# First query tiles of four batches ahead, then batch 0 by tiles of 128 queries, then twelve pairs: a sparse-attention and MLP kernel reordered

## The chip, the cores and the metric

The kernel runs on one core of a Trainium2 chip. Its time is the device time of one launch in microseconds (us): the median of three runs before the change is 282.17 us (280.68 to 282.51). A profile is one execution of the program; its span is counted from the first to the last instruction. TensorE is called PE here, VectorE DVE, ScalarE ACT and GpSimd POOL; SP is the queue that issues most DMAs. PE's weight loads have a row of their own, PEld, and run beside its matmuls.

## What is computed

Two parts follow each other: attention in which each query sees six chunks of 32 keys, and an MLP with a layer norm in front and a residual around it.

```python
# B, H, S, D = 4, 8, 768, 64; chunks of 32 keys, nc = 24
ub = sum(maximum(q * k_min, q * k_max), axis=-1)     # bound of each query against each chunk
ub = where(causal, ub, -1e9)
top_chunks = argsort(ub)[..., -6:]
scores = where(selected chunk and key <= query, q @ k.T / 8, -1e9)
x = softmax(scores) @ v                              # heads side by side: (4, 768, 512)
xn = (x - mean) / sqrt(var + 1e-6) * g_ln
out = x + maximum(xn @ w_ch1, 0) @ w_ch2             # 512 -> 2048 -> 512
```

A query in the first 128 positions has at most four chunks at or before it, so nothing is selected there: it sees all keys up to itself.

## The kernel before

**Tiling.** Queries and keys come in six tiles of 128 per batch. Heads are taken in pairs: 16 pairs, numbered 0 to 15, four to a batch, two heads of 64 channels side by side on 128 partitions. The queries of a batch form two halves of three tiles, r = 0 and r = 1. The MLP works on one half of one batch at a time: 384 rows.

**A pair's way.** q and k are turned so that channels lie on partitions. For batch 0 (pairs 0 to 3) PE does this with fp32 transposes against an identity (`turn`, line 236), half by half; for pairs 4 to 15 the load already brings 32x32 blocks and DVE turns them (line 229). `kbound` takes minimum and maximum of each chunk. `kdiag` puts them into a matrix with the two heads apart. `bounds` multiplies them with the queries on PE: for batch 0 in fp32 with the positive and negative parts of q (line 338), for the others with q split into two fp16 parts (line 325). `select` finds the seventh-largest bound of each row (DVE max instructions, line 356) and writes a 0/1 mask, `maskt` turns the mask on PE (line 366), and `mring` copies it under the queries: `QA`, `QB` hold q in 64 rows and the mask in the other 64, `KA`, `KB` hold k and constant rows of -61440 from `RT`, so that one matmul gives score and mask (`smm`, line 419). `sexp` is the exponential on ACT (line 427), `diag` cuts the diagonal blocks on POOL (line 434), `values` multiplies with v (line 450; v has a column of ones for the sum), `norm` divides on DVE (line 465).

**The MLP.** `pstat` and `centre` compute mean and variance and the centred fp16 rows on DVE (lines 480 to 492); `xt` turns them by a DMA transpose on SP's queue (line 509); `m1` is the first matmul, 16 groups of 128 hidden columns, two groups to a call (line 518); `relu` brings each to SBUF, nearly always on ACT (line 530); `m2` is the second, four calls of four matmuls to a tile of rows (line 543); `fin` scales, adds the residual and issues the store (line 552).

**Order.** The whole order is written out by hand in the string `ORDER`. Each engine and DMA queue takes its instructions in exactly that sequence; `a.b.c@n` calls function `a` with the numbers, and n picks an engine or a count. All PSUM tiles except those of `smm` and `m1` share four buffers (`ps_t`); `smm` and `m1` share two (`ps_m`).

**Fillers.** `busy` (line 117) issues matmuls whose result is overwritten by the next real one, in the calls of batch 0 and its MLP; `warm.11` (line 378) issues eleven such matmuls of 512 columns at the very start.

**Queues.** SP issues loads of q and k, stores, the DMA transposes of `xt` and the copies of `qring`. POOL issues the loads of v and of both weights (each weight in four parts, `w1` and `w2`). Before a weight load POOL writes one element of its target from `kc` (lines 172 and 176), so that the load follows that pair's `kbound`.

Of the kernel before, what the change touches and what calls it, by code (L numbers as in the profile page):

```python
# [10 lines left out]
ALU = mybir.AluOpType  # L11
# [8 lines left out]
def kernel(  # L20
# [19 lines left out]
    TR = NT // NR  # L40
# [19 lines left out]
    vap = ctx.enter_context(tc.tile_pool(name="vap", bufs=5))  # L60
# [3 lines left out]
    xp = ctx.enter_context(tc.tile_pool(name="xp", bufs=5))  # L64
    xcp = ctx.enter_context(tc.tile_pool(name="xcp", bufs=2))
    htp = ctx.enter_context(tc.tile_pool(name="htp", bufs=2))
# [8 lines left out]
    ident_b = const.tile([P, P], BF16, name="ident_b", tag="ident_b")  # L75
    causb = const.tile([P, NT - 1, 2, NCH], BF16, name="causb", tag="causb")
    causf = const.tile([P, NT - 1, 2, NCH], F32, name="causf", tag="causf")
    RT = const.tile([P, S], F16, name="RT", tag="RT")
    tiny = const.tile([1, 1], F32, name="tiny", tag="tiny")
    hsel = const.tile([P, 3, 2], F32, name="hsel", tag="hsel")  # L80
    mhalf = const.tile([P, TR], F32, name="mhalf", tag="mhalf")
    NK = 4
    QA = [ring.tile([P, S], F16, name=f"QA{i}", tag=f"QA{i}") for i in range(NK)]
    QB = [ring.tile([P, S], F16, name=f"QB{i}", tag=f"QB{i}") for i in range(NK)]
    KA = [ring.tile([P, S], F16, name=f"KA{i}", tag=f"KA{i}") for i in range(NK)]
    KB = [ring.tile([P, S], F16, name=f"KB{i}", tag=f"KB{i}") for i in range(NK)]
    NB = 3
    BD = [ring.tile([P, 2, 2, NCH], F32, name=f"BD{i}", tag=f"BD{i}") for i in range(NB)]
    BH = [ring.tile([P, 2, 2, 2, NCH], F16, name=f"BH{i}", tag=f"BH{i}") for i in range(NB)]
    NM = 3  # L90
    MN = [ring.tile([P, NT - 1, P], F16, name=f"MN{i}", tag=f"MN{i}") for i in range(NM)]
# [7 lines left out]
    st = [dict() for _ in range(NG)]  # L99
    hf = {}  # L100
    x_tiles = {}

    other = [0]
    fill = {P: (8, 16, 32), 240: (4, 8, 16), 122: (8, 16, 32)}
# [7 lines left out]
    def busy(o):  # L114
        w = o.shape[1]
        for _ in range((0, *fill[w])[other[0]]):
            nc.tensor.matmul(o, ident_b, causb.rearrange("p s h c -> p (s h c)")[:, 0:w], start=True, stop=True)  # L117

    def consts():
        make_identity(nc, ident_f)
# [10 lines left out]
        nc.gpsimd.memset(causb, 0.0)  # L133
        nc.gpsimd.affine_select(
            out=causb, in_=causb, compare_op=ALU.is_ge, fill=CAUSAL,
            base=P, pattern=[[P, NT - 1], [0, 2], [-CH, NCH]], channel_multiplier=1,
        )
        nc.vector.memset(hsel, 0.0)
        nc.scalar.activation(tiny, hsel[0:1, 0, 0:1], ACTF.Exp)
        nc.vector.memset(hsel[0:64, 0, 1:2], -KS)  # L140
        nc.vector.memset(hsel[64:P, 0, 0:1], -KS)
        nc.vector.memset(hsel[0:64, 1:3, 1:2], KS)
        nc.vector.memset(hsel[64:P, 1:3, 0:1], KS)
        for i in range(NM):
# [552 lines left out]
```

The softmax here doesn't subtract the row's maximum and nothing guards it: scores larger than these inputs give would overflow.

## Time and profile before

| what | value |
|---|---|
| median of three runs | 282.17 us |
| span of the profiled execution | 278.8 us |
| instructions | 6816 |
| HBM read, written | 27.53 MB, 6.29 MB |
| exponentials (line 427) | 96, 84.4 us busy on ACT |
| first MLP matmuls (line 518) | 512, 88.3 us busy on PE |
| second MLP matmuls (line 543) | 400, 93.0 us busy on PE |
| first and last start of line 518 | 45.9 us, 267.8 us |

Busy time is the time in which at least one instruction of a row was under way. Matmuls are pipelined: one of 384 columns shows 326 ns from start to end, but eight in a row take 1.30 us, so the pitch in the chain of waits is used for sums, not the mean duration of one. The median stands 3.4 us above the span.

### The profile page before, as it was taken

The numbers are of one execution on the slowest core, as the hardware profiler recorded it, in microseconds if no ns is written. First come the engines' busy times: TensorE is split into PE (matmuls) and PEld (weight loads), VectorE is DVE, ScalarE is ACT, GpSimd is POOL, SyncE is SP. The second block draws the span as 40 slices with busy tenths as digits, with TensorE's granted clock in tenths as the row PEclk, the third lists the DMA queues.
The fourth block names the chain that finished last, engine by engine and source line by source line (L and its number), as shares of the span: only waits on it lengthen the run. The fifth ranks groups of instructions, "written<-read, shape, count | busy, mean of one in ns | idle before, by whom it ended". The sixth has DMA issues, their size and how long they took to land.

```text
span 278.8 us, 6816 instructions
## 1 busy us (share of the span) xinstructions
PE 269.2 (97%) x2643; PEld 180.1 (65%) x2643; DVE 215.9 (77%) x632; ACT 177.9 (64%) x237; POOL 99.4 (36%) x170
## 2 busy tenths in 40 slices
PE   7989998999999999999999999999999999999994
PEld 3978986677556766666667766566666655555541
DVE  6888999899999989999999989898876665021212
ACT  3877997889947856758665787577777332413310
POOL 8615466847292034542262904220164000100100
PEclk9999999999999999999999999999999999999999
DMA  6989999989999995699614799455021012210202
GB/s 150 200 177 170 190 127 199 146 122 178 161 182 144 146 178 126 93 179 189 70 41 96 123 144 120 72 162 105 0 68 40 38 42 72 77 40 38 75 4 114
DMA packets 135745, 32.05 MB, mean 115 GB/s; under 512 B 127008, under 2 KB 132640, under 8 KB 135712
## 3 DMA queue, kind: packets, MB, share of 16 engines
q1 hardware_dynamic: 106320, 24.00, 44.3%
q0 software_dynamic: 29248, 7.34, 28.3%
q8 instruction: 21, 0.34, 0.5%
q10 hardware_dynamic: 144, 0.26, 0.3%
q14 instruction: 12, 0.10, 0.1%
HBM read 27.53 MB, written 6.29 MB: 121 GB/s over the span
## 4 chain that ended last, share of the span: by engine, by line
PE 87%; DVE 6%; DMA 3%; ACT 2%; issue 1%; SPq 1%; DVEq 0%; ACTq 0%
PE mm L518 30%; PE yp L543 30%; PE mm L419 11%; PE sm L450 6%; PE ub L325 3%; DMA xT<-xc 2%; PE junk L378 2%; PE trh L366 1%; ACT pt L427 1%; PE tr L236 1%; PE ub L338 1%; PE ub L117 1%; DVE bst L480 1%; PE tr L117 1%; DVE x L465 1%; DMA raw<-in_q_dram 1%
## 5 line engine op out<-in xcount | busy, mean ns | idle before, releaser
L427 ACT ACTIVATE pt<-mm 128x1024 f16<-128x1024 f32 (+2 forms) x96 | 84.4, 916 | 22.1 <-PE mm L419 19.9
L543 PE MATMUL yp<-w2b,hT 128*128 128x512 f16 (+2 forms) x400 | 93.0, 370 | 0.0
L518 PE MATMUL mm<-xT,w1b 128*128 128x384 f16 x512 | 88.3, 326 | 1.3 <-DMA xT<-xc 1.3
L530 ACT ACTIVATE hT<-mm 128x768 f16<-128x768 f32 x61 | 49.2, 810 | 61.3 <-PE mm L518 61.0
L518 PEld LDWEIGHTS <-w1b 128*128 128x128 f16 x512 | 49.4, 98 | 34.9 <-issue 1.4
L543 PEld LDWEIGHTS <-hT 128*128 128x128 f16 x400 | 37.3, 98 | 33.2
L434 POOL TENSOR_SCALAR_AFFINE_SELECT pt<-pt 128x768 f16<-128x768 f16 x32 | 29.9, 940 | 50.5 <-ACT pt L427 50.3
L552 DVE SCALAR_TENSOR_TENSOR ot<-yp,rstd,x 128x512 f32<-128x512 f32 (+2 forms) x25 | 17.9, 720 | 31.1 <-PE yp L543 17.7
L419 PE MATMUL mm<-QA,KA 128*128 128x128 f16 (+2 forms) x224 | 34.0, 246 | 0.9 <-ACT pt L427 0.7
L419 PE MATMUL mm<-QB,KB 128*128 128x128 f16 (+2 forms) x224 | 34.0, 246 | 0.0
L503 POOL TENSOR_TENSOR rstd<-ve,mhalf 128x3 f32<-128x3 f32 x8 | 7.0, 880 | 54.2 <-DVE ve L500 54.2
L450 PEld LDWEIGHTS <-pt 128*128 128x128 f16 x672 | 23.9, 98 | 1.8
L450 PE MATMUL sm<-va,pt 128*128 128x65 f16 x672 | 25.0, 193 | 0.0
L419 PEld LDWEIGHTS <-KA 128*128 128x128 f16 x224 | 18.1, 98 | 9.7 <-issue 1.4
L308 POOL TENSOR_TENSOR kc<-kc 128x24 f32<-128x24 f32 x12 | 4.8, 402 | 50.0 <-DVE kc L289 47.9
L419 PEld LDWEIGHTS <-KB 128*128 128x128 f16 x224 | 17.9, 98 | 3.8 <-issue 0.4
L480 DVE BATCH_NORM_STATS2 bst<-x 128x6 f32<-128x128 f32 x96 | 20.1, 274 | 0.0
L465 DVE TENSOR_TENSOR x<-sm,rden 128x384 f32<-128x384 f32 x32 | 17.8, 558 | 1.1
L492 DVE SCALAR_TENSOR_TENSOR xc<-x,mv,gall 128x512 f16<-128x512 f32 x24 | 17.6, 785 | 1.2 <-DMA xT<-xc 1.2
L213 POOL DMA_DIRECT2D va<-in_v_dram x16 | 12.7, 795 | 0.0
L206 POOL DMA_DIRECT2D va<-in_v_dram x12 | 12.7, 1058 | 0.0
L256 DVE SCALAR_TENSOR_TENSOR q<-qnT,q 128x640 f16<-128x640 f32 x12 | 10.8, 899 | 2.0 <-ACT q L253 1.9
(100 smaller groups left out, 351.0 us busy)
## 6 DMA issues: line engine op xcount, KB each, us to landing
out_dram<-ot SPq DMA_DIRECT2D x23, 256.0 KB, 2.1
qnb<-in_q_dram SPq DMA_DIRECT2D x48, 96.0 KB, 3.5
knb<-in_k_dram SPq DMA_DIRECT2D x48, 96.0 KB, 3.0
va<-in_v_dram POOLq DMA_DIRECT2D x12, 192.0 KB, 5.9
w1b<-in_moe_w_ch_dram POOLq DMA_DIRECT2D x4, 512.0 KB, 7.2
w2b<-in_moe_w_ch_dram POOLq DMA_DIRECT2D x4, 512.0 KB, 7.8
raw<-in_k_dram SPq DMA_DIRECT2D x16, 96.0 KB, 3.8
raw<-in_q_dram SPq DMA_DIRECT2D x16, 96.0 KB, 3.6
```

The lines of the kernel that those rows point to most:

```text
L206: nc.gpsimd.dma_start(va[:, :, :, 0:D].rearrange("p h t d -> p (h t) d"), v[b, 2 * hp:2 * hp + 2].rearrange("h (t p) d -> p (h t) d", p=P),)
L419: nc.tensor.matmul(sc[:, hh, o:o + w * P], ks[:, t * P:(t + 1) * P], qs[:, s * P:(s + w) * P], start=True, stop=True,)
L427: nc.scalar.activation(st[g]["pt", r][:, 4 * i:4 * i + o].rearrange("p n h x -> p h n x"), st[g]["sc", r, i][:, :, 0:o * P].rearrange("p h ...
L434: nc.gpsimd.affine_select(out=dv, in_=dv, compare_op=ALU.is_ge, fill=0.0, base=0, pattern=[[0, 2 * TR], [1, P]], channel_multiplier=-1,)
L450: nc.tensor.matmul(pv[:, hh, s2, :], pt[:, where[t, s], hh, :], va[:, hh, t, 0:D + 1], start=(t == 0), stop=(t == s),)
L465: nc.vector.tensor_tensor(xh(b, r)[:, :, 2 * hp:2 * hp + 2, :].rearrange("p s h d -> p h s d"), pv[:, :, :, 0:D], rden.to_broadcast([P, 2, ...
L480: nc.vector.bn_stats(half(b, r)["st"][:, i, hp], xh(b, r)[:, i, 2 * hp:2 * hp + 2].rearrange("p h d -> p (h d)"),)
L492: nc.vector.scalar_tensor_tensor(h["xc"][:, i, :], xs, h["mv"][:, i, 0:1], gall, op0=ALU.subtract, op1=ALU.mult,)
L518: nc.tensor.matmul(hp_[:, i, 0:TR * P], w1b[:, kt, (m + i) * P:(m + i + 1) * P], h["xT"][:, kt], start=(kt == 0), stop=(kt == KT1 - 1),)
L530: nc.scalar.activation(h["hT"][:, m:m + 2], h["hp", m][:, :, 0:TR * P], ACTF.Relu, scale=HS)
L543: nc.tensor.matmul(h["yp", i][:, cs], h["hT"][:, kt, i * P:(i + 1) * P], w2b[:, kt, cs], start=(kt == 0), stop=(kt == KT2 - 1),)
L552: nc.vector.scalar_tensor_tensor(ot[:, cs], h["yp", i][:, cs], h["rstd"][:, i:i + 1], xh(b, r)[:, i].rearrange("p h d -> p (h d)")[:, cs], ...
```

## The change

Attention and MLP are cut in another way, and `ORDER` is new (949 entries for 928).

- **First tiles of all batches.** Tile 0 of each batch, which needs no selection, is done first for all eight heads at once: one load of k and one of q for each batch (`lda`), four fp32 transposes on PE for each (`turna`), scores by 64-row matmuls without a mask (`smma`), one exponential of 1024 columns (`sexpa`), one value product, one norm. `kbounda` leaves that tile's chunk bounds in `kcs`, where the pairs find them later.
- **Batch 0 by tiles.** Tiles 1 to 5 of batch 0 are loaded (`ldt`), turned on PE (`turnt`), bounded and selected (`boundst`, `selectt`) for all eight heads of one tile at a time. q is split into two fp16 parts as for the other batches; the fp32 bounds are gone. `kdiagt` builds four chunks of all four pairs' matrices on POOL.
- **Twelve equal pairs.** Pairs 4 to 15 load, turn and bound tiles 1 to 5 only: 640 columns where there were 768.
- **Halves.** A pair's queries are now two tiles (1, 2) and three tiles (3, 4, 5).
- **MLP.** There are ten units: units 0 and 1 hold tile 0 of two batches each, units 2 to 9 the two or three tiles of a batch's halves. A unit of two tiles takes four groups of 256 columns to an `m1` call and one `relu` of 1024 columns. Units 0 and 1 are turned on PE (`xtp`) and copied by ACT (`xtc`); the others by DMA as before. The hidden rows lie in buffers of four groups (`htp`, eight of them).
- **Gone.** All fillers (`busy`, `warm` in `ORDER`), the bf16 causal constants, the one-element writes before weight loads. No entry of the new `ORDER` has an `@`, so every choice of engine is the first one.

In the new order POOL copies the constant rows for tile 0 (`rows0`) and later issues the weight loads `w1.2`, `w1.0`, `w1.1`, `w1.3` between other work; ACT's queue issues the loads of q for tile 0.

```diff
--- before.py
+++ after.py
...
-    TR = NT // NR
+    LO, HI = (1, 3), (3, NT)
+    NQ = NT - 1
+    SQ = NQ * P
+    NC4 = P // CH
...
-    vap = ctx.enter_context(tc.tile_pool(name="vap", bufs=5))
+    vap = ctx.enter_context(tc.tile_pool(name="vap", bufs=4))
...
-    xp = ctx.enter_context(tc.tile_pool(name="xp", bufs=5))
+    xp = ctx.enter_context(tc.tile_pool(name="xp", bufs=3))
     xcp = ctx.enter_context(tc.tile_pool(name="xcp", bufs=2))
-    htp = ctx.enter_context(tc.tile_pool(name="htp", bufs=2))
+    htp = ctx.enter_context(tc.tile_pool(name="htp", bufs=8))
...
-    def busy(o):
-        w = o.shape[1]
-        for _ in range((0, *fill[w])[other[0]]):
-            nc.tensor.matmul(o, ident_b, causb.rearrange("p s h c -> p (s h c)")[:, 0:w], start=True, stop=True)
...
+    def rrows(i):
+        eng = pick(nc.vector, nc.scalar, nc.gpsimd)
+        copy(eng, KA[i][64:P, :], RT[0:64, P:S])
+        copy(eng, KB[i][0:64, :], RT[0:64, P:S])
+
+    def rows0():
+        eng = pick(nc.gpsimd, nc.vector)
+        eng.tensor_copy(KA0[64:P], RT[0:64, 0:P].unsqueeze(1).to_broadcast([64, NG, P]))
+        eng.tensor_copy(KB0[0:64], RT[0:64, 0:P].unsqueeze(1).to_broadcast([64, NG, P]))
...
-        nc.gpsimd.tensor_copy(w1b[0:1, 0, c.start:c.start + 1], st[g]["kc"][0:1, 0, 0:1])
         nc.gpsimd.dma_start(w1b[:, :, c], w1_r[:, :, c])
 
...
+    def lda(b, nm):
+        if "raw" not in sa[b]:
+            sa[b]["raw"] = xp.tile([P, 2, H, D], F32, name="rawa", tag="x2" if b == B - 1 else "x3")
+        t = sa[b][nm] = sa[b]["raw"][:, 0 if nm == "kn" else 1]
+        eng = nc.sync if (nm == "kn") != bool(other[0]) else nc.scalar
+        eng.dma_start(t, (k if nm == "kn" else q)[b, :, 0:P].rearrange("h p d -> p h d"))
+
+    def ldva(b):
...
+    def ldt(s, nm):
+        t = sb[s][nm] = ldp.tile([P, H, D], F32, name=nm + "t", tag="raw")
+        eng = nc.scalar if other[0] else nc.sync
+        eng.dma_start(t, (k if nm == "kn" else q)[0, :, s * P:(s + 1) * P].rearrange("h p d -> p h d"))
...
+    def turnt(s, nm):
+        ps = sb[s][nm + "T"] = ps_t.tile([P, HP, P], F32, name="tr", tag="one")
+        src = sb[s][nm].rearrange("p (n h) d -> p n (h d)", h=2)
+        for hp in range(HP):
+            nc.tensor.transpose(ps[:, hp], src[:, hp], ident_f)
...
+    def kdiagt(s):
+        c = slice(s * NC4, (s + 1) * NC4)
+        kc = kcs[:, 0:HP, :, c]
+        nc.gpsimd.tensor_tensor(kc[:, :, 1], kc[:, :, 1], kc[:, :, 0], ALU.subtract)
+        bd = smp.tile([P, HP, 2, 2, NC4], F32, name="bdt", tag="bdt", bufs=1)
+        for a in range(2):
+            nc.gpsimd.tensor_tensor(
...
+            nc.gpsimd.tensor_copy(BHr[:, :, a, 0, :, c], bd[:, :, a])
+            nc.gpsimd.tensor_tensor(BHr[:, :, a, 1, :, c], bd[:, :, a], BHr[:, :, a, 0, :, c], ALU.subtract)
...
+    def boundst(s):
+        ub = sb[s]["ub"] = ps_t.tile([P, HP, 2, 2, NCH], F32, name="ub", tag="one")
+        w = (s + 1) * NC4
+        for n in range(HP):
+            for e, (nm, arr) in enumerate((("qh", 0), ("ql", 0), ("rh", 1), ("rl", 1))):
+                nc.tensor.matmul(
+                    ub[:, n, :, :, 0:w], sb[s][nm][:, n], BH[n][:, arr, :, :, 0:w], start=(e == 0), stop=(e == 3),
...
+    def kbounda(b):
+        view = sa[b]["knT"].rearrange("p n (c e) -> p n c e", e=CH)
+        out_ = kcs[:, b * HP:(b + 1) * HP, :, 0:NC4]
+        nc.vector.tensor_reduce(out_[:, :, 0], view, axis=AX.X, op=ALU.min)
+        nc.vector.tensor_reduce(out_[:, :, 1], view, axis=AX.X, op=ALU.max)
...
+    def smma(b):
+        sc = sa[b]["sc"] = ps_m.tile([P, 2, 512], F32, name="mm", tag="mm")
+        for hp in range(HP):
+            for hh in range(2):
+                c = slice(hh * D, hh * D + D)
+                nc.tensor.matmul(
+                    sc[:, hh, hp * P:(hp + 1) * P], (KB0 if hh else KA0)[c, b * HP + hp], sa[b]["qa"][c, hp],
+                    start=True, stop=True,
+                )
...
+    def sexpa(b):
+        pt = sa[b]["pt"] = ptp.tile([P, HP, 2, P], F16, name="pta", tag="pta", bufs=1)
+        nc.scalar.activation(
+            pt.rearrange("p n h x -> p h n x"), sa[b]["sc"].rearrange("p h (n x) -> p h n x", x=P),
+            ACTF.Exp, scale=SCALE / QS,
+        )
...
+    def valuesa(b):
+        pv = ps_m.tile([P, 2, 512], F32, name="mm", tag="mm")
+        sa[b]["pv"] = pv[:, :, 0:HP * (D + 1)].rearrange("p h (n d) -> p h n d", d=D + 1)
+        for hp in range(HP):
+            for hh in range(2):
+                nc.tensor.matmul(
+                    sa[b]["pv"][:, hh, hp, :], sa[b]["pt"][:, hp, hh, :], va0[:, b * H + 2 * hp + hh, 0:D + 1],
+                    start=True, stop=True,
+                )
...
-        a, z = TR * r, TR * r + TR
+        a, z = (LO, HI)[r]
         segs = [(t, t, 1) for t in range(a, z)] + [(t, t + 1, z - 1 - t) for t in range(z - 2, a - 1, -1)]
-        segs += [(t, a, TR) for t in range(a)]
+        segs += [(t, a, z - a) for t in range(a)]
...
-        if i == 0:
-            nb = sum(w for one in bins for _, _, w in one)
-            st[g]["pt", r] = ptp.tile([P, nb, 2, P], F16, name=f"pt{r}", tag=f"pt{r}")
         sc = st[g]["sc", r, i] = ps_m.tile([P, 2, 512], F32, name="mm", tag="mm")
-        if g < HP:
...
+    def tiles_of(u):
+        if u < 2:
+            return [(2 * u, 0), (2 * u + 1, 0)]
+        b, r = divmod(u - 2, 2)
+        return [(b, s) for s in range(*(LO, HI)[r])]
...
+    def xtp(u):
+        h = hf[u]
+        pm = h["xp"] = ps_t.tile([P, KT1, nt(u) * P], F16, name="xq", tag="one")
+        for i in range(nt(u)):
+            for kt in range(KT1):
+                nc.tensor.transpose(pm[:, kt, i * P:(i + 1) * P], h["xc"][:, i, kt * P:(kt + 1) * P], ident_h)
+
+    def xtc(u):
+        h = hf[u]
+        h["xT"] = xcp.tile([P, KT1, nt(u) * P], F16, name="xT", tag="xT")
+        copy(pick(nc.scalar, nc.vector), h["xT"], h["xp"])
+
...
+    def per(u):
+        return 4 if nt(u) == 2 else 2
+
+    def m1(u, m):
+        h = hf[u]
+        w = nt(u) * P
         hp_ = h["hp", m] = ps_m.tile([P, 2, 512], F32, name="mm", tag="mm")
-        if b == 0:
-            busy(hp_[:, 1, 0:240])
-        for i in range(2):
+        for i in range(per(u)):
+            o = (i % (per(u) // 2)) * w
...
+    END = (9, 2)
     ORDER = """
...
-        consts ld.0.0 warm.11 rrows.2.1@1 rrows.0.0 ld.1.0 rinit.3 turn.0.qn.0 rrows.3.1 rinit.1 rinit.2 rinit.0
...
+        ident rows lda.0.kn masks small lda.0.qn rrows.3 turna.0.kn rrows.1 kbounda.0 ldt.1.kn ldt.2.kn ldt.1.qn
+        turna.0.qn lda.3.kn turnt.1.kn qcopya.0 kcopyt.1 kcopya.0 rows0 turnt.2.kn turnt.1.qn turna.3.kn
+        ldt.2.qn smma.0 qhit.1 lda.1.qn kboundt.1 lda.1.kn turnt.2.qn idh kdiagt.0 kboundt.2 qlot.1 caus
+        kcopyt.2 gain qhit.2 turna.1.kn ldva.0 ones ldva.3 lda.3.qn kdiagt.1 qrelt.1 kcopya.3 sexpa.0 lda.2.kn
+        qlot.2 kdiagt.2 rrows.0 qrelt.2 boundst.1 ldva.1 diaga.0 selectt.1 kcopya.1 turna.1.qn boundst.2
+        valuesa.0 kbounda.3 masktt.1 selectt.2 qringt.2 mringt.1 ldvt.2 qcopya.1 smma.1 lda.2.qn masktt.2
+        turna.3.qn norma.0 qringt.1 ldva.2 sexpa.1 diaga.1 turna.2.kn qcopya.3 valuesa.1 kcopya.2 turna.2.qn
+        smma.3 sexpa.3 mringt.2 norma.1 smm.3.0.0 qcopya.2 ldt.4.kn pstata.0 ldvt.1 sexp.3.0.0 smm.1.0.1
+        sexp.1.0.1 diaga.3 turnt.4.kn smma.2 w1.2 valuesa.3 pstata.1 ldt.4.qn kbounda.2 sexpa.2 centre.0
+        diag.3.0 norma.3 diaga.2 ldt.3.kn rrows.2 xtp.0 smm.1.0.0 kboundt.4 smm.3.0.1 sexp.3.0.1 w1.0 values.3.0
+        kbounda.1 sexp.1.0.0 smm.2.0.0 valuesa.2 xtc.0 w1.1 diag.1.0 norma.2 w1.3 values.1.0 smm.2.0.1 norm.1.0
+        pstata.2 sexp.2.0.0 smm.0.0.1 pstata.3 sexp.2.0.1 sexp.0.0.1 ldt.3.qn turnt.4.qn diag.2.0 qhit.4 w2.0
+        smm.0.0.0 sexp.0.0.0 centre.1 diag.0.0 values.2.0 kcopyt.4 kdiagt.4 m1.0.8 norm.3.0 qlot.4 values.0.0
+        norm.2.0 turnt.3.kn kboundt.3 relu.0.8 norm.0.0 xtp.1 pstat.1.0 turnt.3.qn kdiagt.3 m1.0.0 qrelt.4
+        qhit.3 pstat.3.0 pstat.2.0 xtc.1 relu.0.0 qlot.3 ldt.5.kn m1.1.8 boundst.4 half_ m1.1.4 selectt.4
+        qringt.4 ldt.5.qn kcopyt.3 w2.1 relu.1.8 m1.0.4 masktt.4 pstat.0.0 turnt.5.kn relu.1.4 rstd.0 relu.0.4
...
+        m2.7.0.3 m2.7.1.2 values.15.1 xt.8.0 m1.8.4 norm.15.1 m1.8.12 relu.8.4 pstat.15.1 relu.8.12 m1.8.8
+        m1.8.0 m2.7.2.3 centre.9 relu.8.8 xt.9.0 relu.8.0 xt.9.1 xt.9.2 m2.7.1.3 rstd.8 m2.8.1.0 m1.9.8 fin.7.2
+        m1.9.14 m2.8.0.0 m2.8.1.1 relu.9.14 m1.9.0 m2.8.0.1 relu.9.8 fin.7.1 m2.8.1.2 relu.9.0 m1.9.2 relu.9.2
+        rstd.9 m2.8.1.3 m1.9.6 m1.9.10 relu.9.6 m1.9.12 fin.7.0 relu.9.12 m2.9.0.0 m2.9.1.0 m1.9.4 relu.9.4
+        fin.8.1 m2.8.0.2 m2.8.0.3 relu.9.10 m2.9.0.1 m2.9.0.2 fin.8.0 m2.9.0.3 m2.9.2.0 fin.9.0 m2.9.2.1
+        m2.9.1.1 fin.9.2.0 m2.9.1.2 m2.9.1.3 fin.9.1 m2.9.2.2 m2.9.2.3 fin.9.2.1
```

## The prediction

> **What bounds the kernel now.** I read the busy shares first, then the slices, then the chain of waits in order of time, then busy time by stretches.
>
> ```profile
> PE 269.2 (97%) x2643; PEld 180.1 (65%) x2643; DVE 215.9 (77%) x632; ACT 177.9 (64%) x237; POOL 99.4 (36%) x170
> ...
> PE   7989998999999999999999999999999999999994
> ...
> DVE  6888999899999989999999989898876665021212
> ```
>
> PE is the bound on average, but DVE is full too up to about two thirds of the span. Which one leads in which stage needs the stretches (columns: PE, PEld, DVE, ACT, POOL busy, clock, DMA share, GB/s):
>
> ```profile
> 0.00:46.00 46.00, 41.09 (x463) 35.23 (x464) 40.55 (x144) 36.46 (x67) 25.35 (x47) 1.00 1.14 172
> 46.00:66.70 20.70, 19.84 (x254) 14.38 (x254) 19.11 (x63) 17.14 (x23) 14.68 (x28) 1.00 1.05 149
> 66.70:275.00 208.30, 208.29 (x1930) 130.52 (x1927) 155.54 (x426) 124.31 (x149) 59.35 (x96) 1.00 0.62 99
> ```
>
> From 66.7 us to 275.0 PE never stops; then 3.8 us of last `fin` and store remain. All that can be lost lies before 66.7 us. There PE looks busy, but the chain shows with what:
>
> ```profile
> 1.85 4.79 PE junk L378 x11
> ...
> 9.58 0.89 PE ub L338 x8
> 10.47 1.79 PE tr L117 x32
> ...
> 40.93 4.87 DMA xT<-xc
> 45.93 4.06 PE mm L518 x24
> 49.99 0.69 PE ub L325 x20
> ...
> 64.42 0.92 PE sm L450 x30
> ...
> 77.91 1.30 PE mm L518 x8
> 79.21 0.86 PE yp L543 x4
> ```
>
> L378 and L117 are fillers. These rows also give the pitches: 162.5 ns for 384 columns (1.30/8), 215 for 512 (0.86/4), 30.6 for 65 (0.92/30), 34.5 for a bounds matmul (0.69/20), 111 for an fp32 one (0.89/8), 56 for 128 columns (1.79/32).
>
> **PE's real work before.** `m1` 512 at 162.5 = 83.2 us; `m2` 82.9; scores 448 matmuls, 86,016 columns, 37.0; `values` 672 at 30.6 = 20.6; bounds 8.3 in pairs 4 to 15 and 9.5 in batch 0; 80 mask turns 4.5; 48 fp32 turns at 110 ns 5.3. Sum 251.1. Check: 208.3 of it falls after 66.7 us, so 42.8 before. I call **loss** the span without real work and tail: 278.8 - 251.1 - 3.8 = 23.9 us, of which 10.2 are `busy` (80 x 56 ns + 56 x 102 ns), 4.8 `warm`, the rest waits. The change can win at most this and what it saves in real work.
>
> **What the Trainium skill says.** "TensorE: Matmul & The Clock Gate", section "Wait — 56ns, not 53.3ns?": a warm matmul costs N/2.4 ns plus 2.5; all pitches from 128 columns up agree, so 256 columns, which the trace lacks in a row, cost 109 ns. Same page, "Part 1: The HAM clock gate": PE runs at half rate until some 3.4 us of activity, and again after an idle window of that length. The junk row agrees: 4.79/11 = 435 ns for 512 columns against 215 later. "SBUF — State Buffer", "Who interferes with whom": DVE copies in the two-port mode and POOL instructions exclude each other for a whole instruction. The trace shows it: the cast to `ident_h` took 841 ns beside a POOL instruction, that to `ident_b` of equal size 164.
>
> **The change on PE.** `m1`: 384 at 109.2 + 256 at 162.5 = 83.5. `m2` 82.9. Scores: 20 blocks for 21 in each pair, 35.2, and `smma` 32 at 56 ns, 1.8; no trace row has 64-row matmuls, so 0.9 if two run side by side, 2.5 if each switch costs 20 ns more. `values` and `valuesa` 20.6. Bounds 8.3, and `boundst` 80 at 30 ns, 2.4: 7 us won against fp32. Mask turns 4.5. fp32 turns 72 at 110 ns, 7.9: 2.6 lost. `xtp` 0.9. Sum **248.0**, 3.1 less. Fillers gone: -15.0 of PE time, which is worth nothing unless real work takes their place.
>
> **The change on DVE.** Priced by the rows: pair turns and `kbound` at 640 columns save 3.9 + 3.3; `rrows`, `kdiag`, `relu`, `qhi` no longer on DVE save 8; `qlot`, `qrelt`, `qringt` add 12; `kbounda`, `kboundt` (nine times two reductions of 512, 0.68 us each) add 3.4, the rest about 1. I summed the rows along both orders: 223.3 us before, 221.6 after, as good as unchanged. Measured before are 215.9 (neighbours overlap a little), so I multiply DVE sums by 0.967. ACT stays as it was (184.5 and 182.6 by the same sums). POOL gets some 20 us more (six `kdiagt` of seven instructions at 0.38 us, `rows0` 4.3) and stays below both in total; only the start matters there.
>
> **The start.** Before the first `m1` (`m1.0.8`) PE has only 14.0 us of work in the new order. Its time is set by two chains. DVE: 23.7 us up to the end of `centre.0`, plus waits of about 6 (nothing to reduce before data arrives at about 6.3, as the first turn at 6.47 shows; then for POOL), so 30; `xtp` and `xtc` add 1.5; 32. POOL: identity and `RT` end at 4.1 us as before, `rows0` two copies of 2,048 elements by the row of 834 ns for 768, three `kdiagt` 8.0, v loads at 0.8 to 1.06, three `diaga` at 1.2: 27.0 us before `w1.2` is issued, so at 28 at the earliest. Its landing took 6.3 us at least, median 7.2: 35 to 36. `values.2.0` stands before it on PE and waits for exponential and `diag` until 36. So `m1.0.8` starts at 36 to 37, loss 22 there, instead of 45.9 for the first `m1` before, where PE had done 25.3 real (loss 20.6). The DMA transpose of 4.87 us is gone from the path, yet PE had less to do up to there. Then `boundst.4` waits for `qrelt.4`: +1. From there `m1`, `m2` of units 0 to 2 are ready, loss 23.
>
> **What is late next.** From the sums along the order DVE is ahead of PE in work by 180.3 - 164.0 = 16.3 us at `norm.10.1` (16.5 at `norm.8.1`); before, the largest was 88.1 - 70.2 = 17.9 at `norm.4.1`. If D is the time that DVE has stood idle up to there, the end is 248.0 + 16.5 + D + 3.8 = **268.3 + D**; by PE alone it is 251.8 + loss. Both count, the larger wins; they cross at D = 6.5. Before, DVE had idled 11.8 us by `norm.10.1` (started at about 162.5, work 150.7). I take the same 11.8, and 2 for the ports: POOL is full in the first 38 us, where it was 25.35 in 46, and `rrows`, `idh`, `qringt` are SBUF copies of the kind that is held up. D = 13.8, span 282.1. The cold clock without fillers (14 us of PE work at half rate: between 0, hidden behind DVE, and +7) sits in the same D; new waits on the four `ps_t` buffers, which four open `m2` tiles fill at once after `m2.2.1.0`, likewise, 0 to 6. Removing one-element writes saves POOL 8 x 0.18 and frees nothing else.
>
> The executions' median lies 3.4 us above the profile's span; I add it: **285.5 us**.
>
> **Rivals.**
> 1. *The start is worth what it was meant to be* (ends faster): DVE idles only in the first 20 us, D = 6, so PE's loss of 18 to 26 decides. Span 251.8 + 23 = 274.8, time 278.2; best case 273 with loss 18. For it: DVE lead is 1.4 us lower than before, 7 us of fp32 bounds are gone. It decides if D stays below 10.
> 2. *Cancelled*: D about 11, time 279.4 to 285.0; fillers, fp32 bounds and later first rows balance.
> 3. *Starved buffers*: PE, in order, waits at `masktt` and `bounds` for a free `ps_t` buffer held by an open `yp`. Four such waits of 2 to 3 us in 66 to 200 us give 293 to 296. Against it: before, none is seen after 66.7 us with as many buffers.
> 4. *The weights come late*: w1 and w2 are issued within some 20 us beside loads at 172 GB/s. If each part takes 10 us (the longest seen for w2), `m1.0.4` and `m2.0.0.2` wait 5 more: 283 to 290 by itself.
>
> **Chances.** Within 1% (279.35 to 285.0) is what a measurement of this kernel can't tell from no change. Forecast with rivals 3 and 4, slower: 0.48 (0.10 of it above 293). Rival 2: 0.22. Rival 1: 0.30. Signs are mixed; the likeliest case's own range is 282 to 291. The 8-in-10 range takes rival 1 to its floor and most of rival 3: 273 to 295.
>
> **What would show it.** Filler rows gone, `m1` of 256 columns at 1.75 us for 16. First `m1` at 36 to 37 us: right; at 30, POOL's chain was shorter; past 42, port or weights. DVE waiting under 8 us by pair 10 and PE full from 45 on speaks for rival 1; PE idle after 66 us with DVE full, for the forecast; PE idle with DVE idle too, for rival 3. The first scores at twice the pitch show the cold clock. Wrong would be the forecast if real PE work differed from 248 by over 4 us.

## The result and the profile after

The kernel after the change takes 295.94 us (median of 4 runs, 295.11 to 296.29), the kernel before it 281.43 on the same chip: **ratio 1.0521, interval 1.0475 to 1.0568**, slower. The profiled execution took 296.29, its span is 294.6 us. The forecast was 285.5 in a range of 273 to 295: the direction was right, the size was not. The median lies 14.5 us above before's. Ratios and intervals here and below are taken from the executions outside a slower state into which some fall, so that they can differ a little from the quotient of two medians.

The lines of after's page that answer to those of before, and with them the granted clock and the DMA engines (tenths in 40 slices of 7.4 us):

```profile
PE 263.3 (89%) x2680; PEld 183.5 (62%) x2680; DVE 217.8 (74%) x627; ACT 175.6 (60%) x223; POOL 109.3 (37%) x209
...
PE   3658789991999997999899989998999999999995
...
DVE  6989999733859899999999999999974238331122
...
PEclk9855799997799999999999999999999999999999
DMA  9999897198948799994889438145922102032012
```

DVE's work is what it was (217.8 against 215.9). In the slices, counted from 0, it has a dent that before did not have: 8 to 11, from 59 to 88 us. PE has one too (the 1 in slice 9). And in slice 7, just ahead of the dent, the DMA engines stand nearly idle. By stretches (columns: length, then PE, PEld, DVE, ACT, POOL busy, clock, DMA share, GB/s; the DMA share adds up the time of packets and can come out above 1):

```profile
0.00:40.00 40.00, 25.60 (x248) 20.08 (x249) 35.69 (x86) 22.24 (x34) 27.96 (x55) 0.74 1.27 180
40.00:62.60 22.60, 22.10 (x221) 18.17 (x219) 19.37 (x66) 13.13 (x17) 10.46 (x29) 1.00 0.75 103
62.60:74.10 11.50, 5.03 (x49) 3.56 (x47) 2.68 (x15) 1.81 (x3) 0.00 (x0) 0.82 1.00 153
74.10:100.00 25.90, 25.61 (x287) 18.21 (x287) 19.54 (x50) 19.39 (x22) 10.02 (x18) 0.95 0.75 118
100.00:200.00 100.00, 94.94 (x1086) 65.42 (x1086) 98.03 (x294) 76.11 (x99) 43.18 (x78) 1.00 0.78 120
200.00:295.00 95.00, 90.06 (x796) 58.08 (x795) 42.47 (x122) 42.89 (x51) 17.67 (x29) 1.00 0.27 54
```

The third row is a hole: in 11.5 us PE works 5.0, DVE 2.7, ACT 1.8 and POOL nothing. Only the DMA engines are busy. The chain of waits (start, length, what) tells what everybody waits for:

```profile
51.91 3.51 PE mm L670 x32
...
56.83 1.25 SPq L646
...
58.13 0.58 SPq L202
...
59.37 2.35 SPq L202
...
61.76 9.57 DMA qnb<-in_q_dram
...
71.35 0.85 DVE qnT L405
```

Pair 4's q (`ldb.4.qn`, line 202) is issued from 58.1 us on and has landed at 71.3. `turn.4.qn` (line 405) waits for it on DVE, and behind it in DVE's order stands `selectt.5`, for whose mask PE waits. There are two suspects. SP's queue, then the weights of POOL's queue (start, length of the issue, what, number of DMA instructions):

```profile
20.76 1.61 SPq L219 DMA_DIRECT2D qnt<-in_q_dram  x1
55.48 2.60 SPq L646 DMA_TRANSPOSE xT<-xc  x2
58.13 7.97 SPq L202 DMA_DIRECT2D qnb<-in_q_dram  x4
66.14 5.34 SPq L202 DMA_DIRECT2D knb<-in_k_dram  x4
71.53 2.15 SPq L202 DMA_DIRECT2D qnb<-in_q_dram  x4
```

```profile
57.59 1.54 POOL L185 DMA_DIRECT2D w2b<-in_moe_w_ch_dram  x2
```

**SP's order:** from 22.4 to 55.5 us the queue does nothing, and the loads stand behind `xt.2.1`. That one waits for `centre.2` up to 52.3, and then 3.1 us more for the last first product of unit 0 (`m1.0.12`), whose `xT` buffer it takes over. **The DMA engines:** half a microsecond before the loads POOL issues `w2.2` and `w2.3`, 1 MB; the four DMA instructions of `qnb` then take 7.97 us to issue, where 2.15 is usual. The Trainium skill, "Trainium Kernel Development and Optimization", section "Key Constraints", says that transfers issued from SP, ACT and POOL share the same 16 engines; the DMA share of 1.00 in the hole fits that. So an earlier start or free DMA engines could each be the remedy. The experiments take them apart.

### The profile page after: what moved, and what is told of

Same layout as the page of the kernel before. It is cut to its first block, busy times and chain, and to the rows that moved or that the text cites. A ratio compares the mean times of both kernels' runs of the same rounds, so it can differ in the third digit from the quotient of the medians.

```text
span 294.6 us, 6890 instructions
## 1 busy us (share of the span) xinstructions
PE 263.3 (89%) x2680; PEld 183.5 (62%) x2680; DVE 217.8 (74%) x627; ACT 175.6 (60%) x223; POOL 109.3 (37%) x209
## 4 chain that ended last, share of the span: by engine, by line
PE 50%; DVE 24%; DMA 10%; SPq 8%; POOL 3%; issue 2%; ACT 2%; DVEq 0%; POOLq 0%
PE mm L670 21%; PE yp L699 17%; SPq L202 6%; PE mm L534 6%; DMA qnb<-in_q_dram 4%; PE sm L568 3%; DVE xc L629 3%; DMA knb<-in_k_dram 2%; DVE ot L708 2%; DVE qnT L405 2%; DVE m L477 1%; DVE q L418 1%; DMA out_dram<-ot 1%; DVE QB L117 1%; DVE knT L405 1%
## 5 line engine op out<-in xcount | busy, mean ns | idle before, releaser
L670 PE MATMUL mm<-xT,w1b 128*128 128x256 f16 (+1 forms) x640 | 90.3, 296 | 2.6 <-DMA xT<-xc 1.5
L670 PEld LDWEIGHTS <-w1b 128*128 128x128 f16 x640 | 62.2, 99 | 25.1 <-issue 2.0
L686 ACT ACTIVATE hT<-mm 128x768 f16<-128x768 f32 (+1 forms) x56 | 49.7, 900 | 44.2 <-PE mm L670 40.4
L553 POOL TENSOR_SCALAR_AFFINE_SELECT pt<-pt 128x512 f16<-128x512 f16 (+1 forms) x32 | 25.5, 802 | 69.7 <-ACT pt L545 69.6
L640 POOL TENSOR_TENSOR rstd<-ve,mhalf 128x2 f32<-128x2 f32 (+1 forms) x10 | 8.3, 828 | 47.1 <-DVE ve L637 43.4
L212 POOL DMA_DIRECT2D va<-in_v_dram x24 | 21.4, 894 | 0.7 <-issue 0.5
L581 DVE RECIPROCAL rden<-sm 128x4 f32<-128x4 f32 (+1 forms) x32 | 5.6, 176 | 17.9 <-PE sm L568 17.9
L405 DVE STREAM_TRANSPOSE qnT<-qnb 128x640 f32<-128x640 f32 x12 | 10.0, 831 | 9.9 <-DMA qnb<-in_q_dram 9.9
L415 ACT ACTIVATE q<-qnT 128x640 f16<-128x640 f32 x12 | 8.8, 736 | 13.8 <-DVE qnT L405 13.3
L582 DVE TENSOR_TENSOR x<-sm,rden 128x256 f32<-128x256 f32 (+1 forms) x32 | 15.7, 491 | 1.1
```

The source lines that it names most:

```text
L212: nc.gpsimd.dma_start(va[:, hh, :, 0:D], v[b, 2 * hp + hh, P:S].rearrange("(t p) d -> p t d", p=P))
L405: nc.vector.transpose(t, st[g][nm].rearrange("p c e -> p (c e)"))
L553: nc.gpsimd.affine_select(out=dv, in_=dv, compare_op=ALU.is_ge, fill=0.0, base=0, pattern=[[0, 2 * (z - a)], [1, P]], channel_multiplier=-1,)
L670: nc.tensor.matmul(hp_[:, i // (per(u) // 2), o:o + w], w1b[:, kt, (m + i) * P:(m + i + 1) * P], h["xT"][:, kt], start=(kt == 0), stop=(kt ...
L686: nc.scalar.activation(o, i, ACTF.Relu, scale=HS)
```

## The experiments

D is, as in the prediction, the time that DVE stands idle; I read it up to 200 us. Ratios are to the kernel before on the same chip, with intervals; before's median was between 279.9 and 281.4 in the various comparisons. Each edit is of the change's kernel unless another is named; what moves in the order is shown with its neighbours.

### SP's order, or the DMA engines

The loads ahead of `xt.2.1`:

```diff
 ldt.5.qn
+ldb.4.qn ldb.4.kn ldb.5.qn ldb.5.kn
...
-ldb.4.qn
 turn.4.qn
-ldb.4.kn
...
```

> The four loads of pairs 4 and 5 (ldb.4.qn, ldb.4.kn, ldb.5.qn, ldb.5.kn) are put into SP's queue ahead of the two transposing transfers of unit 2 (xt.2.1, xt.2.0), nothing else. Theory A, SP's queue was held: it sat idle from 22.4 to 55.5 us behind xt.2.1, which waited for centre.2, so the loads landed at 71. Now they are issued as turnt.4 and turnt.3 free their buffers (30 to 50 us) and land before 60; turn.4.qn no longer stands in front of selectt.5; of the 11.5 us from 62.6 to 74.1 in which PE did 5.0 us of work, 5 to 7 come back, and the loads of pairs 6 and 7 move up as well. Time 286 to 290. Theory B, the DMA engines were full (w2.2 and w2.3, 1 MB, issued at 57.6 just before them): the same hole closes too, but the loads now meet w1.0, w1.1, w1.3 and w2.0 between 33 and 46 us, and these come later, first m1 after 40 us instead of 39.0; 291 to 295. Theory C, the start alone cost the time (clock of 0.59 and 0.55, DVE slowed beside POOL): no change above 1 us, 295 to 296.

Measured: 290.44 us, 1.0328 (1.0254 to 1.0403). The time lies between the ranges of theories A and B. The hole is gone, PE works 20.0 of 20 us from 60 to 80. The first `m1` starts at 40.6 instead of 39.0, as theory B had said, but that decides nothing: with SP's order left alone it starts at 38.4 in the next run and at 40.2 in the one without a megabyte below. Two readings remain: the loads are early, and they are also out of the weights' way.

Only the weights ahead, SP untouched:

```diff
 w2.1
+w2.2 w2.3
...
 turn.4.qn ldb.4.kn
-w2.2
 m1.2.0
-w2.3
 qhi.4
```

> Only the last two parts of the second weight (w2.2, w2.3) move, to directly behind w2.1 in POOL's queue, so they are issued at about 47 us instead of 57.6; SP's order stays. Theory A, SP's queue: pair 4's loads are still issued from 58.1 us; they may take less than the 8.0 us that four descriptors then took, but no more than 3 us of the hole come back: 293 to 296. Theory B, full DMA engines: the four take 2.2 us as they do elsewhere, pair 4's q lands near 62 instead of 71, and 5 to 8 us come back: 288 to 291. Theory C: 295 to 296.

Measured: 288.12 us, 1.027 (1.0215 to 1.0325), half of the loss. The issue and the hole's stretch in this run:

```profile
57.53 2.82 SPq L202 DMA_DIRECT2D qnb<-in_q_dram  x4
60.39 2.66 SPq L202 DMA_DIRECT2D knb<-in_k_dram  x4
```

```profile
60.00:80.00 20.00, 19.34 (x173) 13.58 (x171) 13.30 (x33) 11.26 (x13) 6.65 (x12) 1.00 0.89 118
```

SP holds the loads back as long as in after (57.5 us, 58.1 there), and yet the four issues take 2.8 us instead of 8.0 and PE is full. Theory A alone is out. But the loads' own move helped too, so both were joined.

> Both moves at once: pair 4's and 5's loads ahead of xt.2.1, and w2.2, w2.3 directly behind w2.1. Theory A2, there was one hole and each move alone closes it (the loads and the last megabyte of weights must not meet after 57 us, whichever of the two goes first): the gains of 5.5 and 7.8 us do not add, 286 to 289, and what is left is PE full from 50 to 80 us while DVE waits for it. Theory B2, two separate losses, one on SP's queue and one in the DMA engines: they add, 281 to 284. Against both, the traffic of 1 MB more between 30 and 57 us makes w1 or w2.1 late: 289 to 293.

Measured: 293.16 us, 1.0458 (1.0393 to 1.0523). Neither A2 nor B2; the third possibility comes nearest, but w1 and w2.1 are not what is late. SP's queue here:

```profile
45.08 5.98 SPq L202 DMA_DIRECT2D qnb<-in_q_dram  x4
51.15 8.69 SPq L202 DMA_DIRECT2D knb<-in_k_dram  x4
60.02 2.59 SPq L646 DMA_TRANSPOSE xT<-xc  x2
```

The loads now meet the weights at 47 us. What comes late is `xt.2.1`, at 60.0 instead of 55.5, because the last load's issue holds SP's queue for 8.7 us; PE then waits 2.4 us for `xT`, and `boundst.5`, behind it on PE, lets DVE wait 5.0. The same transfers collide with another victim. The view of the DMA engines, in slices of 1 us from 36 to 76, shows both; first after, then this run:

```profile
DMA  9999999999106991000014797979999977188999
```

```profile
DMA  9999999999999899899999999998000000000000
```

In after the engines idle from 51 to 56 us and are then full when the load is urgent; here they are full without a break up to 63.

Last, the traffic itself was taken away, with each order of SP. These two kernels leave out the second half of the second weight and read the first half twice, so that they compute something else; all other instructions stay:

```diff
-w2.2
 m1.2.0
-w2.3
...
-                h["yp", i][:, cs], h["hT", kt // 4][:, kt % 4, i * P:(i + 1) * P], w2b[:, kt, cs],
+                h["yp", i][:, cs], h["hT", kt // 4][:, kt % 4, i * P:(i + 1) * P], w2b[:, kt % 8, cs],
```

> The kernel after with 1 MB less to fetch: w2.2 and w2.3 are left out, and the second product reads the first half of the second weight twice (its result is then another); every other instruction and the order stay. Theory A3, the collision in the DMA engines makes the hole: with nothing issued at 57.6, pair 4's q lands at 61 to 63 although SP is held just as before, and the time is 286 to 289, as with the megabyte fetched 11 us earlier (288.1). Theory A, SP's queue held behind centre.2 makes it: 292 to 296. Theory E, DMA engines bound the whole front, and a megabyte less is worth its 4.7 us everywhere: 4 to 6 us below the run with early weights, 282 to 284.

> The same megabyte left out, and pair 4's and 5's loads ahead of xt.2.1. Theory A3: nothing collides in either order, so SP's order is worth little by itself; within 2 of the run before it, 285 to 289. Theory A: SP's order is worth 5 to 9 us here too: 286 to 289 where the run before it takes 292 to 296. Theory F, the loads ahead cost something by themselves (they met w1 and w2.0, and the time with both moves was 293.2): 1 to 4 us above the run before it.

Measured: 288.29 (1.0273, 1.0202 to 1.0343) and 288.08 us (1.0251, 1.0194 to 1.0308). Theory A3 is right in both: without the megabyte SP's order is worth nothing, and leaving the megabyte out is worth no more than fetching it 11 us earlier. Theories A, E and F fall. **The collision of `w2.2`, `w2.3` with pair 4's loads costs 7 to 8 us** (7.7 and 7.8 by the medians, 7.0 by the ratios), about half of the loss. Whether the two meet in the DMA engines themselves or in what feeds them, no run separates. The longest time from issue to landing of a `qnb` piece between 20 and 100 us, in after and in the run without the megabyte in the same order of SP:

```profile
DMA to landing us min/median/max: 2.3/2.8/11.8
```

```profile
DMA to landing us min/median/max: 2.3/2.9/3.6
```

### The start: clock, shared ports, transfers

Three parts of the start were suspects of the prediction. The fillers put back, as matmuls of 128x512 into a tile that nothing reads (it takes one of the two `ps_m` buffers):

```diff
 turnt.1.qn
+warm.4
...
 turna.1.kn
+warm.5
...
+warm.4
 valuesa.0
```

> Thirteen matmuls of 128 by 512 into an unused PSUM tile are added in PE's gaps between 9 and 20 us; nothing else. Theory C, the cold clock is a term of its own: the granted clock of 10 to 30 us rises from 0.57 to about 1, the first m1 comes 1.5 to 3 us earlier than 39.0, and the time falls by 1.5 to 3 us. Theory A, DVE sets the end of the start (8.9 and 9.7 of 10 us busy there): the clock rises all the same, but the time stays within 1 us of 296, because the fillers stand in front of PE work that DVE waits for or because the hole at 62.6 swallows what was won.

`rows0` taken from POOL:

```diff
-        eng = pick(nc.gpsimd, nc.vector)
+        eng = pick(nc.gpsimd, nc.vector, nc.scalar)
...
-rows0
...
+rows0@2
 sexpa.1
```

> Only rows0 moves: from POOL at 3.9 to 7.9 us to ACT, ahead of sexpa.1 at about 20 us. Theory C: the two 64x640 copies of DVE that took 1.92 and 1.93 us beside it take 0.32 again, kbounda.0 starts at 5.9 to 6.5 instead of 8.3, centre.0 about 2 us earlier than 30.0, and the time falls by 2 to 3 us. Theory A: the start gains 1 to 2 us, which the hole at 62.6 swallows or passes on: 294 to 296, because pair 4's loads wait for centre.2 and that moves up by what DVE gains, at most 2.

Measured: 296.23 (1.0558, 1.0503 to 1.0613) and 296.63 us (1.0571, 1.0515 to 1.0628): neither gains anything. The mechanisms themselves were seen. With the fillers the clock from 10 to 20 us is 1.00 instead of 0.59, and PE is 1.1 us ahead at `smma.1` (20.6 us, 21.8 in after). Then it waits for batch 1's v, which comes 1.1 us later than in after (after first, then with fillers):

```profile
25.89 0.60 PE L384 MATMUL mm<-va,pta 128*128 128x65 f16 x8 [0.65 <-DMA va<-in_v_dram]
```

```profile
27.03 0.60 PE L384 MATMUL mm<-va,pta 128*128 128x65 f16 x8 [4.13 <-DMA va<-in_v_dram]
```

The clock also varies without fillers: in the run without a megabyte and with SP's order left alone, whose order is after's up to 57 us, it was 1.00 from 10 to 30 us, and the first `m1` started at 40.2, not earlier than after's 39.0. In after, two of DVE's four copies lie beside POOL's (timeline of DVE, then of POOL):

```profile
3.86 0.32 DVE L117 COPY KA<-RT 64x640 f16<-64x640 f16 x1 [1.69 <-POOL RT L134]
4.20 1.92 DVE L117 COPY KB<-RT 64x640 f16<-64x640 f16 x1
6.13 1.93 DVE L117 COPY KA<-RT 64x640 f16<-64x640 f16 x1
```

```profile
3.90 2.04 POOL L175 COPY KA<-RT 64x2048 f16<-64x2048 f16 x1
5.99 1.89 POOL L176 COPY KB<-RT 64x2048 f16<-64x2048 f16 x1
```

With `rows0` on ACT all four take 0.32 and `kbounda.0` starts at 6.1 instead of 8.3. The 2 us are then lost in front of batch 1's values: DVE waits 2.25 us at 26.9, PE 2.65 for `va`. To see whether transfers bound the start, the order of the transfers was changed too, on top of the early weights and `rows0` on ACT:

```diff
 ldva.3
+ldva.1
...
 ldva.2
+ldvt.2
...
+gain
 lda.2.qn
```

> On top of the early w2.2 and w2.3 (288.1): rows0 to ACT as before, and the order of the start's transfers changed so that ldva.1 goes out directly behind ldva.3, ldvt.2 behind ldva.2, and the gain row before lda.2.qn instead of before ldva.0. Theory A2, the start is bound by its transfers (DMA engines full from 2 to 30 us; where DVE was freed early, it then stood 2.3 to 3.0 us for the values of batch 1): with va of batch 1 there by 22, the 2 us that rows0 gives at 8 us reach centre.0, which starts at 27.5 to 29 instead of 29.9; 285.5 to 287.5. Theory C2, the start's time is made by the chain DVE, POOL, PE itself, or doesn't matter for the end: within 1 of 288.

Measured: 289.13 us, 1.0325 (1.0278 to 1.0373): no gain over the early weights alone. Half of the expectation came: `centre.0` moves from 29.9 to 27.4. Then DVE stands still for the next data:

```profile
27.36 1.41 DVE L629 SCALAR_TENSOR_TENSOR xc<-x,mv,gall 128x512 f16<-128x512 f32 x2
32.13 0.21 DVE L392 RECIPROCAL rdena<-mm 128x8 f32<-128x8 f32 x1 [3.36 <-PE mm L384]
```

PE in turn had waited 3.04 us for batch 2's q, which now lands later. In after the DMA engines are full from 3 to 30 us and move 6.38 MB in the first 36 (6.32 in before); what was fetched sooner in this run made something else late. Two more runs put the clock to the test where no hole hides it, and in the kernel before:

```diff
 w2.1
+w2.2 w2.3
...
 turnt.1.qn
+warm.4
...
```

> Early w2.2 and w2.3 (ratio 1.027 to the kernel before), with the thirteen fillers of 9 to 20 us. If the cold clock is worth in the new order what it was worth in the old one (2.3 us, ratio 1.0083), and only the hole hid it when the fillers alone were added: ratio 1.017 to 1.022, 285 to 286.5. If DVE and the transfers set the first 50 us, so that PE's clock there doesn't matter: 1.025 to 1.03, within 1 us of 288.

Measured: 288.63 us, 1.0291 (1.0253 to 1.0328): nothing is won.

The kernel before without its fillers:

```diff
-        for _ in range((0, *fill[w])[other[0]]):
+        for _ in range(0):
...
-warm.11
```

> The kernel before without its fillers: warm.11 and all matmuls of busy (17.4 us of PE time by its trace, all but 0.8 of it before 40 us) left out, nothing else. The prediction counted the loss of the fillers at 0 to 7 us. If the clock is a cost of the change: the granted clock falls below 0.8 in 10 to 40 us here too and the time rises by 2 to 5 us, 283 to 287. If PE has slack at the start: within 1 of 281.

Measured: 282.94 us, 1.0083 (1.0054 to 1.0111), 20 runs: 2.3 us, with a clock of 0.50 from 20 to 30 us and the first product at 48.4 us instead of 45.9. So the lost fillers have a price in the old order. In the new one no run shows it.

### The other half: order behind the hole

Without the collision the kernel is still 2.5 to 2.7% above the kernel before. In the run with early weights DVE idles 6.7 us between 60 and 80 while PE is full there (19.34 of 20, shown above), and from 100 to 200 PE idles 5.2 us while DVE is full (98.0). The idea to be tried: the new order puts three units' products in front of pairs 4 and 5. Seven runs tried to trade one for the other.

```diff
 masktt.3
-m2.0.1.1 m2.0.0.1 mringt.3 qrelt.5
...
+m2.0.1.1 mringt.3 turn.4.qn qrelt.5 m2.0.0.1 relu.1.12 relu.1.0 boundst.5 qhi.4 m1.2.0 turn.4.kn selectt.5 rstd.2 masktt.5
+qlo.4 kbound.4 m1.2.4 relu.2.0 kdiag.4 mringt.5 qrel.4 m2.0.1.2 relu.2.4 turn.5.qn m1.2.8 bounds.4 m2.0.0.2 qhi.5 relu.2.8
...
```

> f1's two moves, and the stretch from m2.0.1.1 to smm.3.1.2 put in another order: boundst.5, selectt.5, turn.4, kbound.4, bounds.4, select.4 go ahead of units 0 and 1's second products, m2.1.0.0 and m2.2.1.0 behind m1.2.12, the two fin.0 of DVE behind turn.5.kn, and pair 7's and 6's loads ahead of them on SP. Theory A2, DVE idle up to norm.10.1 sets the end (268.3 + D): D in 50 to 80 us, 9.2 in the run with early weights, falls to 3 to 5, and the time to 282 to 285. Theory D2, PE is full in that stretch anyway and its sum sets the end: 287 to 289.

> f3 and f2's changes of the start together. Theory A2: 280 to 283, the sum of both gains. Theory C2 and D2: 287 to 289.

Measured: 290.01 (1.0374, 1.0299 to 1.045) and 290.93 us (1.0396, 1.0346 to 1.0447), above the ranges of all theories. That is less than the 293.16 of the two moves that they build on, with overlapping spreads, but not less than the early weights alone. DVE's idle time in 60 to 80 falls to 2.3 us, and 6.4 come back in 80 to 90, where DVE has nothing left and waits 5.6 us for pair 1's values. A second rewriting gave DVE pair 5's bounds and pair 0's values to do there:

```diff
...
+smm.0.1.0 rstd.1 ldvt.3 select.4 sexp.0.1.0 m2.0.1.3 qlo.5 turn.5.kn smm.0.1.1 smm.0.1.3 ldvt.5 sexp.0.1.1 ldb.7.kn ldb.6.qn ldb.7.qn
+qrel.5 kbound.5 sexp.0.1.3 m2.0.0.3 fin.0.1 smm.0.1.2 kdiag.5 maskt.4 sexp.0.1.2 diag.0.1 kcopy.4 fin.0.0 m1.2.12 values.0.1 mring.4
+bounds.5 relu.2.12 norm.0.1 qring.4 smm.1.1.0 select.5
...
```

> Pair 4's and 5's loads first as in the first experiment, w2.2 and w2.3 left where the change has them, and the stretch from m2.0.1.1 to smm.3.1.2 rewritten so that DVE has work in it: bounds.4 and select.4 early, pair 0's second scores ahead of pair 1's so that kcopy.4, mring.4, qring.4 and bounds.5, select.5 can follow at once, m2.1.0 and m2.2.1 behind them. The end is 268.3 + D; the first experiment had D of 7.8 up to 60 us and 7.3 in 60 to 100. If DVE's idle time in 60 to 100 is only a question of order: 2 to 3 us of it left, and 284 to 286. If DVE merely waits later for the PE work that was put back (as in the first rewriting, 6.4 us in 80 to 90): 288 to 291.

> The run before it with the thirteen fillers of 9 to 20 us. There the clock was 0.50 from 20 to 40 us with the loads first; if that is a cost once the hole at 62 is gone, PE reaches 50 us with more done and the time falls by 1 to 3 us below the run before it; if DVE and the transfers set the start, within 1.

Measured: 293.31 (1.0449, 1.0396 to 1.0502) and 293.54 us (1.0475, 1.04 to 1.0551). The first lies above both of its ranges. Again the wait only moves: 10.5 us of idle DVE between 80 and 100, behind products that had been put back; PE is full there. Then unit 2's products were moved by 20 to 30 us:

```diff
-m1.2.0 relu.2.0 m1.2.4 relu.2.4 m1.2.8 relu.2.8 m1.2.12 relu.2.12
...
 smm.4.1.0
+sexp.4.1.0 m1.2.0 relu.2.0
...
 m2.1.1.1
+m1.2.8 relu.2.8
 smm.4.1.1
+sexp.4.1.1 m1.2.4 relu.2.4
 maskt.5
+m1.2.12 relu.2.12
...
 m2.2.0.3
+m2.2.1.0
```

> The early w2.2, w2.3 (288.1), and unit 2's share of the feed-forward part taken out of the stretch of 62 to 80 us: its first product (m1.2.0 to m1.2.12, 7.3 us of PE) goes to behind pair 4's second scores, where PE stood at about 95 us, and m2.2.1 and fin.2.1 (3.5 us of PE) behind m2.2.0. Theory G, the new order puts three units' products in front of pairs 4 and 5 while DVE has nothing to do (6.7 us of D in 60 to 80): D falls by 4 to 6, PE gets the work back where it waited for DVE (5 us of idle time from 100 to 200), and the time is 282 to 284.5. Theory H, DVE's time is not to be had there (pair 4's bounds and values wait for their own chain of ACT, POOL and transfers, or the loads of pairs 6 and 7 come late behind fin.0): 287 to 289.

> The run before it, with three loads of pairs 7 and 6 moved ahead of the two stores of fin.0 on SP's queue, directly behind ldb.5.kn. If DVE now runs out of loaded data because SP holds these loads behind fin.0: 1 to 3 us below the run before it. If not: within 1 of it.

> The run before it with the start's changes (rows0 to ACT, ldva.1, ldvt.2 and the gain row in the other order). Theory A2, transfers bound the start: DVE is freed of 3.4 us of slow copies and waits as much longer for batch 1's and 2's data, within 1 of the run before it. Theory C: 2 to 3 us below it.

Measured: 296.04 (1.0558, 1.0494 to 1.0623), 294.04 (1.0504, 1.043 to 1.0579) and 293.66 us (1.0472, 1.0416 to 1.0529): all worse than the early weights alone. The first fits neither theory. The second is 2.0 us below it, with overlapping spreads; the third, within 1 us of the second, is what A2 had said. In the first of them DVE's wait in 60 to 100 hardly changes (7.4 us against 7.6), and 6.1 us come anew before 104 us (DVE's timeline, then ACT's):

```profile
104.31 0.83 DVE L418 SCALAR_TENSOR_TENSOR q<-qnT,q 128x640 f16<-128x640 f32 x1 [6.09 <-DMA knb<-in_k_dram]
```

```profile
102.49 1.02 ACT L686 ACTIVATE hT<-mm 128x1024 f16<-128x1024 f32 x1 [1.00 <-PE mm L670]
103.54 0.74 ACT L415 ACTIVATE q<-qnT 128x640 f16<-128x640 f32 x1
```

The releaser named, `knb`, had landed before 97.4, when DVE turned it; what ended the wait is ACT's `qhi.7` of 103.5. It stands behind the moved `relu.2.12`, which waits for PE. That is a fault of this edit, so the runs don't refute theory G; they show only that this move is no remedy.

Last, the loads of pairs 7 and 6 ahead of `fin.0`'s stores, with the early weights:

```diff
 ldb.5.kn
+ldb.7.kn ldb.6.qn ldb.7.qn
...
```

> Early w2.2 and w2.3, and three loads of pairs 7 and 6 ahead of the two stores of fin.0 on SP's queue. If SP's order costs something here (these loads went out from 76 to 85 us, DVE's turn.7 and turn.6 follow at 84 to 100): 1 to 2 us below 288, ratio 1.020 to 1.024. If loads are there in time in both orders, as the run with less traffic says of pair 4's: within 1 us, 1.025 to 1.03.

Measured: 288.35 us, 1.0273 (1.023 to 1.0316): nothing is won. No version beat the kernel before; the best that computes the same is the change with early weights.

## Why the prediction was right in sign and wrong in size

D by stretches, from busy time of DVE in each profile, beside the prediction's 268.3 + D. The prediction counts D up to `norm.10.1`; in the new order that starts at 198.6 to 208.3 us, so that 200 is near enough (24.8 in after up to it, 24.7 up to 200). In before it starts at 162.5, with D of 11.7 up to there.

| run | span | D to 60 | 60 to 100 | 100 to 200 | D | span - (268.3 + D) |
|---|---|---|---|---|---|---|
| after | 294.6 | 7.5 | 15.2 | 2.0 | 24.7 | +1.6 |
| loads first | 288.9 | 7.9 | 7.3 | 3.9 | 19.1 | +1.5 |
| weights first | 286.3 | 7.5 | 7.6 | 2.0 | 17.1 | +0.9 |
| both | 291.4 | 8.0 | 11.9 | 1.8 | 21.8 | +1.3 |
| a megabyte less | 286.3 | 8.2 | 7.0 | 2.0 | 17.2 | +0.8 |
| second rewriting | 290.8 | 7.5 | 12.2 | 1.8 | 21.4 | +1.1 |
| unit 2 later | 295.6 | 8.2 | 7.4 | 9.4 | 25.0 | +2.3 |
| before | 278.8 | 6.8 | 0.8 | 8.2 | 15.8 | own order |

The stretch that makes the difference, in after and then in before (columns as above, DVE third after the length):

```profile
60.00:100.00 40.00, 33.24 (x351) 23.39 (x349) 24.75 (x68) 22.64 (x26) 10.02 (x18) 0.91 0.83 124
```

```profile
60.00:100.00 40.00, 39.13 (x455) 26.34 (x451) 39.21 (x117) 31.44 (x38) 17.90 (x35) 1.00 1.19 158
```

1. **"The end is 268.3 + D": right.** In all fourteen kernels of the new order with `rows0` on POOL the span lies 0.0 to 2.3 us above it; in the four with `rows0` on ACT, where DVE has about 4 us less work, 1.9 to 3.1 below. From the start of `norm.10.1` to the end all eighteen take 87.0 to 87.3 us (268.3 - 180.3 = 88.0 by the prediction's sums): what they differ in comes before it. The sum held for causes that the prediction had not thought of.
2. **"I take the same 11.8, and 2 for the ports. D = 13.8": this step failed.** D was 24.7, 10.9 more. With the +1.6 of item 1, and -2.1 because the median lies 1.3 us above the profile's span and not 3.4, that is the whole way from 285.5 to 295.9. The new order does not inherit before's waits: to 60 us they are alike (7.5 and 6.8), from 60 to 100 they are 15.2 against 0.8. 7.6 of these are the collision; D is 17.1 without it, and why that is still 3.3 above 13.8 stays open. With the early weights the kernel takes 288.1, still more than before, so the forecast's sign did not hang on the collision that it missed. The prediction looked at the weights' landing and at POOL's queue but never followed SP's queue through `xt.2.1`, and never asked what the DMA engines carry between 50 and 70 us.
3. **Rival 4, the weights come late, had the right transfers and the wrong victim.** Parts of w2 did take long (median 9.3 us in after), but `m2` didn't wait; the loads issued behind them did.
4. **Rival 3, starved PSUM buffers: not seen, though its sign was.** PE and DVE do stand idle together in the hole. But the long wait of PE there, 6.5 us before `masktt.5`, is for DVE's mask.
5. **The start: right within 3 us.** `centre.0` ended at 32.2 (30 said; it started at 29.96), `w1.2` issued at 30.18 (28 at the earliest), first `m1` at 38.98 (36 to 37). The port term measured 3.2 us (2 said) and was worth nothing in time: what it freed was spent waiting for transfers.
6. **The cold clock, 0 to +7 in D:** the low end. 2.3 us in the old order, none seen in the new, with fillers or in an execution that was warm without them.
7. **The pitches: right.** 32 matmuls of 256 columns took 3.51 us, 110 ns each (109 said), and the 64-row pairs of `smma` ran side by side, both starting at 11.43.
8. **Slips that change nothing.** PE's terms for before add up to 251.3, not 251.1. The DVE terms that are listed add 1.2 us, the row sums take off 1.7; measured are 1.9 more. Both casts that were read as blocked and unblocked lie beside the same POOL instruction (2.12 to 3.23 us), so they show nothing; the copies of 1.92 and 0.32 us do.

**Open:** the remaining 2.5 to 2.7%. Shown is where it lies, 7.6 us of idle DVE from 60 to 100 us under a nearly full PE (38.6 of 40), 5.2 of idle PE from 100 to 200 under a full DVE. That a better order of that stretch would win it is argued only; the rewritings tried here did not.

## What to carry to other kernels

When work is moved to the front, list what each DMA queue holds there and what the DMA engines carry in every 10 us, not only when each load is issued: a load that is needed at once must not follow a megabyte that is needed later. A sum like "fixed work plus the idle time of the leading engine" can be exact and still useless if the idle time is copied from the old order; price it stretch by stretch in the new one. Before curing a wait at the start, see whether the next transfer would be there.

## What the hardware showed that was not expected

- **The issue of a load lasts longer when the DMA engines are full.** Four issues of `qnb` or `knb` on SP took 2.15 us in free stretches, 7.97 beside 1 MB of weights and 8.69 beside 1.5 MB. What stands behind them in SP's queue waits with them: `xt.2.1` went out at 60.0 us in that last run, at 55.5 in after. The Trainium skill, "Perfetto Trace Analysis", section "DMA Instruction — HWDGE (DVE, Sync)", says that the profiled window of such an instruction covers the making of its descriptors, and that the engines may begin on them before all are made, when the buffer is full; these numbers agree with it, though no run here shows the buffer.
- **Slower copies can be free.** DVE lost 3.2 us to two copies of 1.92 and 1.93 us beside POOL's, and getting them back gave nothing.
